# Causal masks of two heads in one operation, with a new written order, in a decay attention with a gated MLP

## The chip, the cores and the metric

The kernel runs on one core of one Trainium2 chip. The metric is device time in microseconds (us) of one launch, median of repeated runs.

## What is computed

Attention with a decay over 8 batches of 8 heads (sequence S = 576, head size D = 64), then an MLP on the heads put side by side (512 columns) that is gated by a causal convolution of 5 taps:

```python
log_f = np.log(np.clip(f, 0.0001, 1.0))
cum = np.cumsum(log_f, axis=-1)
decay = cum[:, :, :, None] - cum[:, :, None, :]
scores = np.where(causal, -1000000000.0, scale * q @ k.T + decay)
attn = np.exp(scores - max); attn = attn / (sum + 1e-09)
x = (attn @ v) of all heads, as (batch, 576, 512)
...
gate_pre[s] = sum over k of conv_w[k] * x[s - 4 + k]
out = (sigmoid(gate_pre) * (x @ w_val)) @ w_out
```

(The listing is shortened: q, k, v, x and f are inputs, `max` and `sum` run over a row of scores, `causal` is the part above the diagonal.)

## The kernel before

**Work.** Two heads make a pair; there are 32 pairs (i = 0 to 31), four to a batch. The 576 rows of scores of a head are cut into four blocks of 128 (j = 0 to 3; block j has 128(j+1) columns because of the causal mask) and a tail of 64 rows, which the two heads of a pair share as one block of 128 rows ("l"). For each pair the steps are:

- Scores on PE (helper `mm`, line 246), in three groups: blocks 3 and 2 of both heads, blocks 1 and 0, the tail. From pair 4 on q and k are split in a rounded high part Xh (line 261) and a rest Xl (line 375), and three products are added.
- The decay of a head, one row of 512 numbers, is read from a small table in DRAM and broadcast to 128 partitions, into one of four tiles dm (two pairs' worth); the tail has its own tile dl. The mask is put into the same tile: of the last 128 columns of block j (128j to 128j+127) those above the diagonal get a large negative number. Lines 468 (POOL, affine_select) and 470 (DVE, an addition of the constant tile tri4, in the rows tri) are this step, one operation for each head and block. The step of block j overwrites columns that block j+1 reads unmasked. So it comes after the reduction of block j+1 of that head.
- Line 459, DVE: a custom reduction adds dm to the scores in PSUM and finds the row's extreme, negm. Line 463, ACT: the exponential, with its row sums zs. Lines 477 and 478, DVE: 1/z for the pair.
- Line 503, PE: transposes of the probabilities in three groups (block 3; blocks 2 and 0; block 1); line 527: those of the tail, with 1/z in the same operation. Copies to SBUF by ACT or DVE (helper, line 261).
- 1/z goes out to DRAM (rzd, issued by SP on line 272) and comes back, broadcast to 64 partitions for each head, into one of three tiles x32.
- Products with V on PE, in two halves; line 577, DVE: each half times 1/z in x32, in place. That is x of the MLP.
- x is split in xh (line 261, ACT or DVE) and xl (line 584, POOL or DVE). The convolution is a first product (line 266, 267 or 268, on ACT, POOL or DVE) and four taps (line 619, DVE); for the first four pairs a tap may be on POOL instead, as a product (line 268) and an addition (line 617). Then a tanh for the gate on ACT.
- Per batch: products with w_val (PE), line 651 the gate times the product into h (DVE), its split hh and hl (lines 261 and 665), products with w_out (PE), line 692 (ACT) or 694 (DVE) to an output tile ot (two of them), and the store.

The start loads and cleans up the weights (a decode in integers on DVE and ACT) while the first pairs run.

**Order.** Nothing runs in the order of this code. Each step is put as a node into `Plan` with the engines that may run it and a cost for each; `Plan.order` then goes through a long string, TABLE (lines 46 to 106), that holds for every node in turn its number, its engine and its PSUM banks (eight of 512 columns). The order of each engine's queue, the engine of each step with a choice, and each bank are thus written out in TABLE; the costs in the code take no part when the kernel is built. The waits between engines follow from the tiles.

The node of the mask, in `plan_s`:

```python
any_("sel", {"POOL": 0.26, "DVE": 0.3}, pp - (0.3 if j == 3 else 0.0), sel, [*dkey, ("tri4",)], dkey)
```

Of the kernel before, what the change touches and what calls it, by code (L numbers as in the profile page):

```python
# [7 lines left out]
F32 = mybir.dt.float32  # L8
# [3 lines left out]
ALU = mybir.AluOpType  # L12
# [4 lines left out]
P = 128  # L17
# [5 lines left out]
L0 = NB * P  # L23
# [8 lines left out]
BIG = 8.0e9  # L32
# [5 lines left out]
NDM = 4  # L38
# [8 lines left out]
0430520q000930240010b30n010l000m010d30a30630e20f10740z40K40g10h20r30i20p000C228001232a02900V40B10D20E22j0450F10G20H20t32R40I20J20c32h22i12d22b22s062m2  # L47
2k20M12f22e10j40N22t02c10o002n12q22644642l12g12o22u22r12D0210x32p12F22x0054042v12A0434245f42E20w30P22B10Q12z12w20O22C12V012672X00R22G030S22W03222y1302
340050U32-22Y23924442H13522Q10X13-42T43315h42K45d40T12Z12_10s33110y33d030Y20-23e00_12I42M42O43724a33b20u33k020Z23f21021125q33c13613g13813i063a13A0055b
44c23l23x0233C13j23h23D045943B13u0063y24843z13m15l33v11333o33E13p23q23r23w14f31211444b023174d23N14o0064i34g21610v34B041f43F44e13Q024l34j24p34m21724s34  # L50
h14k14n14q23H44v34r14t24C24u14y33L43J43O014D17844z27e44L0734A14w24F0454x14M13R24H13P23s24N14E24O063n31821925n37c43S14G13U34P17n13T37l35m050123V23W25o2
4I0435r24S47g44Y15t34K15z0677t35w34J15u21a15x24Q47a45A35s15y15M034W44Z005B25N24U45p18n45D35C15v15O15E24_051b25J25K25G35L15F13X25Q0125H21c25025W0735I17
m34-21d21i25S15P25Y15Z023Y28A18p47o31e31h11k27q35335437p006545j47k36715-18B27r21j25X15T0237w35R17u25_48C37z31l16145525V17x26547A26341m28v47C0715627s15
U11q45113t17v16a037y168027D37B13Z17T0607U15727P048r41n27V16b26928F37E25236e17Q26c16f26g26h27i48D31p37R17J28t47K29C48I37F17G38E063206d36n046k057H21s11o
# [12 lines left out]
hd2h93gp4cF04h41cG0hl05cC1ha2jY4e82hi3hb1iP4fm2iR4cH2hm2cD4g-1j22hj2gw02he1hk1hf3hg2hn1hh1fk2cI4k24gx2gu04e53gv2hp013hv056hs002cK04cL0hr1hu2e92ho2ea2h
y02hq1ht1iZ3fn2hw1i-05017hz2hI2cM1i_3k04hA4j32cN4kb3j02j52j82hx1j62iV2jc2gy1j11gA1hC4jb023hE4kc3k93kh3gB2j92jf3jd2hG4cP06eb1j41ji3cQ0jo04j71jp2cU00jg2
ja1jq1je1cR2fo2jj2jl3hJ07hL06jm2gC2jn1jk1gz3js024hK2jh1jy037jv051gD2jw1hM2jA2ju1jr2jt1ka2lb4j-4hP1jz1jx2hN1fp2k44iT4hV06ke3hO3cV0lq3jB01jC2kd03457hQ2k
f2ki2gE2jL1cW1kn3kq012hY00hZ0kj1lj4ko2kk3lf4hW0lo1lw3ku3i104kg1mq4kl2kr2ks2jD4hR2km1jF4kp1h-2i20kv2hX2jJ4i405kx2gF1ky2h_1fq1i50k83hS2ms4jH4kD06jM00hT2  # L70
kE2i02lp3k64kz1kw1i32i62lr3jO03ld4mD3kt1kF1lh4kA2kB2kH046kC1kN057kJ1mF1i901jP2i72ia0kI1jN2lt3cX4ln2i82kK006kO1kL1ib2kG2mu4ls05423kP2kQ00ic07cS4lx2kR1l
u2kU4lC3jQ2id0k-1ly1lv1lS00lz3ie2lF075lA2if1lD2l104lG3lJ2lB1mE2lK2lT2hU1lP2my4kM1mG2lQ2lU1ig2kS4kW4k_06lH2mI2jS3ih02lR1lM3ii0lE1jR3oy4lN2ij2lI1lL1kY4i
k03il0lW025m0001lO1l02lZ067im2lX1jT2oC4in1ip02ll4jU2l22lV2l-1oN3m11m303m22lY1io3m41mL2mH05106oG4md1mw4oO2mM2m74mU034oL1mN1oT3mJ2mR2mC2iq0l_2mS2mK1l51o
A4mO3mY3mP2iu01mT1l62mZ2n22mQ1mV3jV2ir1mW2iz07pN4l72n505m54is4m_3mX1q02m94oE4iv0iw2m-1n62n32mb4me02n41mg01n71n02jW2n9040nf056oM3nb1oQ3mf2mh2na2iA0n11n
h1q13nc063mk1oP04012l82l32ng1iB2mA4n82p-3oK3nd1ml2ni05oR2ne1ns1p0037nj2oW2l43oU2oX2oS1pT4pd05oZ2ix4o-2p13p43mi1pP4nk4iE04oY1p52pe2o_1oV1nm4pa3pR4pf1iF
0p22pb2mj3p31p73q63nq4mm2p61no4p82nt00r84nu2pc1p91nv05ph030iG2pg2nw2pn047r64pV4nx2pq05mn2ny2pk021po2p_3mo2jX1q33pj1pp1pA1nF07pr1nG0pm1q201456nH2qf070l
92q42q72pl1pi1nI03q92nz1q81qa2qc2q51qd2nJ0nA2qb1qg3nN02nK2iC4qh2la1qi1nL1qj3nO0oI4qs04r24r04nQ03mp1qk2sf4qp2pZ2nB2qe1r44nM2rf3nP2nR0ps4qm3pu4pw4pB01qq
2qr1ss2rg3ql1qn2py4rl3qt2pC2pD02pE2qC006qo1qu1ra4qw017qz045qv2nS2qD2qA2sh4pX4qF02rd3re3qy1nV07pH3qB1iH4rc3qx1st3qG2nT1nU3rh01450qP2ri3su2ru023nC2nW0rm
# [12 lines left out]
A-1CP3CQ2AX1BQ053CD4AW1B14BI2BF2DQ4BN2BO2BU3zh07BK3zp04zq0zi0wL1BL2BG1z81BP1BR3BV2ug4BS2B-3B34B_2BM1zj2BX3xX2BW1zm02zk2C100xY2BJ1By3CW3zn0BY2B74C01C22
# [76 lines left out]
def tile_decay_attention_gated_mlp(  # L168
# [27 lines left out]
    def tiles(n, shape, dt, name):  # L196
        return [const.tile(shape, dt, name=f"{name}{j}") for j in range(n)]
# [626 lines left out]
```

## Time and profile before

| | us |
|---|---|
| median of 3 runs | 571.55 (569.11 to 572.59) |
| profiled execution, its own time | 567.13 |
| its span | 565.4 |
| busy: PE, DVE, ACT, POOL | 501.1, 479.9, 342.9, 241.8 |
| mean granted clock, share of full speed | 0.954 |

All durations come from the one profiled execution. The rows are in a section below; a row gives a line of the kernel before, the engine, the operation, the tiles by name (written <- read), and its times. A wait of an engine is idle time just before an instruction, with what released it. Two engines are busy for more than four fifths of the span, so the shares do not name one bound, and the stretches and waits are to be read.

### The profile page before, as it was taken

The numbers are of one execution on the slowest core, as the hardware profiler recorded it, in microseconds if no ns is written. First come the engines' busy times: TensorE is split into PE (matmuls) and PEld (weight loads), VectorE is DVE, ScalarE is ACT, GpSimd is POOL, SyncE is SP. The second block draws the span as 40 slices with busy tenths as digits, with TensorE's granted clock in tenths as the row PEclk, the third lists the DMA queues.
The fourth block names the chain that finished last, engine by engine and source line by source line (L and its number), as shares of the span: only waits on it lengthen the run. The fifth ranks groups of instructions, "written<-read, shape, count | busy, mean of one in ns | idle before, by whom it ended". The sixth has DMA issues, their size and how long they took to land. (4 is left out here: it accounts for less than half of the span.)

```text
span 565.4 us, 14142 instructions
## 1 busy us (share of the span) xinstructions
PE 501.1 (89%) x5136; PEld 429.3 (76%) x5136; DVE 479.9 (85%) x1204; ACT 342.9 (61%) x933; POOL 241.8 (43%) x352
## 2 busy tenths in 40 slices
PE   7877897897889998999988989989899778999997
PEld 6655786776888878878877778977798666988795
DVE  5879979989689998889888799898979868987871
ACT  5877756766657666766746556655655545677321
POOL 3337854637272716245463334252434345442000
PEclk9988769999799999999989989989989989999999
DMA  6763634545353653544642754446444345522112
GB/s 236 195 231 122 179 132 128 155 139 200 94 158 117 172 168 118 173 132 137 200 137 83 186 141 139 140 118 194 131 132 122 90 149 152 182 88 69 60 39 93
DMA packets 35014, 79.58 MB, mean 141 GB/s; under 512 B 5056, under 2 KB 5312, under 8 KB 34944
## 3 DMA queue, kind: packets, MB, share of 16 engines
q1 hardware_dynamic: 34864, 78.54, 45.4%
q8 instruction: 40, 0.66, 0.5%
q14 instruction: 30, 0.25, 0.1%
q10 hardware_dynamic: 80, 0.15, 0.1%
HBM read 68.93 MB, written 9.73 MB: 139 GB/s over the span
## 5 line engine op out<-in xcount | busy, mean ns | idle before, releaser
L463 ACT ACTIVATE P<-banks,negm 128x384 f32<-128x384 f32 (+3 forms) x256 | 133.4, 529 | 97.6 <-DVE negm L459 94.7
L468 POOL TENSOR_SCALAR_AFFINE_SELECT dm<-dm 128x128 f32<-128x128 f32 x169 | 60.6, 367 | 189.9 <-DVE negm L459 153.1
L459 DVE CUSTOM_DVE_ANT_0 banks<-banks,dm 128x512 f32<-128x512 f32 (+2 forms) x240 | 115.2, 508 | 16.6 <-POOL dm L468 7.1
L619 DVE SCALAR_TENSOR_TENSOR gate<-x,cw,gate 128x576 f32<-128x576 f32 x126 | 123.5, 985 | 0.6
L246 PE MATMUL banks<-xh,wall 128*128 128x288 f32 x512 | 116.3, 309 | 6.0 <-DVE h L651 1.9
L246 PE MATMUL banks<-pt,vt 128*64 128x128 f32 (+1 forms) x1280 | 100.5, 311 | 16.6 <-ACT ot L692 7.1
L261 ACT COPY pt<-banks 128x512 f32<-128x512 f32 (+1 forms) x173 | 85.8, 540 | 42.9 <-PE banks L503 27.3
L246 PEld LDWEIGHTS banks<-pt,vt 128*64 128x64 f32 x1280 | 80.9, 145 | 29.8 <-ACT P L463 8.1
L246 PEld LDWEIGHTS banks<-xh,wall 128*128 128x128 f32 x512 | 87.4, 194 | 11.2 <-DVE h L651 2.4
L246 PE MATMUL banks<-wall,hh 128*128 128x512 f32 x288 | 92.8, 403 | 2.6 <-ACT ot L692 1.4
L246 PE MATMUL banks<-xl,wall 128*128 128x288 f32 x256 | 77.2, 301 | 0.0
L503 PE MATMUL banks<-ident,P 64*128 64x64 f32 x1280 | 56.3, 235 | 17.5 <-ACT P L463 9.9
L375 POOL TENSOR_TENSOR Xl<-Xr,Xh 128x640 fp32r<-128x640 f32 (+1 forms) x43 | 68.7, 1604 | 2.8 <-DVE Xh L261 2.6
L503 PEld LDWEIGHTS banks<-ident,P 64*128 64x128 f32 x1280 | 48.5, 146 | 27.5 <-ACT P L463 15.4
L246 PEld LDWEIGHTS banks<-wall,hh 128*128 128x128 f32 x288 | 51.0, 188 | 14.9 <-ACT ot L692 1.5
L246 PE MATMUL banks<-Xh 64*128 64x512 f32 (+3 forms) x224 | 54.3, 381 | 5.5 <-DVE x L577 2.4
L246 PE MATMUL banks<-wall,hl 128*128 128x512 f32 x144 | 56.6, 393 | 0.0
L463 ACT ACTIVATION_READ_ACCUMULATOR P<-banks,negm 128x1 f32 x256 | 51.9, 203 | 0.0
L246 PEld LDWEIGHTS banks<-xl,wall 128*128 128x128 f32 x256 | 49.8, 195 | 0.1
L246 PE MATMUL banks<-Xl,Xh 64*128 64x512 f32 (+3 forms) x224 | 49.7, 346 | 0.0
L246 PE MATMUL banks<-Xh,Xl 64*128 64x512 f32 (+3 forms) x224 | 49.6, 345 | 0.0
L577 DVE TENSOR_TENSOR x<-banks,x 128x192 f32<-128x192 f32 (+1 forms) x64 | 27.7, 449 | 17.6 <-DMA x<-rzd 13.4
(102 smaller groups left out, 794.0 us busy)
## 6 DMA issues: line engine op xcount, KB each, us to landing
Xr<-in_x_dram SPq DMA_DIRECT2D x32, 608.0 KB
dm<-decd SPq DMA_DIRECT2D x60, 256.0 KB
vt<-in_v_dram SPq DMA_DIRECT2D x32, 320.0 KB
x<-rzd SPq DMA_DIRECT2D x64, 144.0 KB
out_dram<-ot SPq DMA_DIRECT2D x36, 256.0 KB
dl<-decd SPq DMA_DIRECT2D x60, 144.0 KB
ot<-in_w_val_dram SPq DMA_DIRECT2D x2, 512.0 KB
wu<-in_w_val_dram SPq DMA_DIRECT2D x2, 512.0 KB
```

Of the source, the lines that this page charges most:

```text
L246: nc.tensor.matmul(out, lhsT=lhsT, rhs=rhs, start=start, stop=stop)
L261: (eng.copy if eng is nc.scalar else eng.tensor_copy)(out=out, in_=in_)
L375: eng.tensor_tensor(out=Xl[r][:, a:e], in0=Xr[r][:, a:e], in1=Xh[r][:, a:e].bitcast(F32), op=ALU.subtract)
L459: nc.vector.tensor_tensor_reduce(out=sl, in0=sl, in1=add, op0=ALU.add, op1=ALU.min, scale=-0.125, scalar=3.0e38, accum_out=negm[r][:, col])
L463: nc.scalar.activation(out=dst[:, o:o + ext], in_=bank(key)[:, c0:c0 + ext], func=AF.Exp, bias=negm[r][:, col], scale=-1.0, accum_out=zs[r ...
L468: eng.affine_select(out=t, in_=t, pattern=[[-1, P]], base=0, channel_multiplier=1, compare_op=ALU.is_ge, fill=-BIG)
L503: nc.tensor.transpose(out=bank(key[a])[:, c:c + D], in_=Pt[ms[h]][sl, BOFF[b] + P * j:BOFF[b] + P * j + P], identity=ident[sl, sl])
L577: nc.vector.tensor_tensor(out=o, in0=bank(key)[:, 0:qb - qa], in1=o, op=ALU.mult)
L619: eng.scalar_tensor_tensor(out=gt, in0=src, scalar=wt_, in1=gt, op0=ALU.mult, op1=ALU.add)
```

## The change

1. The four decay tiles of 512 columns become two tiles of two heads each. One operation puts the mask of block j into both heads: 128 partitions by 2x128 columns. It waits until the reductions of block j+1 of both heads have been made.
2. Two costs that the planner knows are changed (the mask, the transposes). They take no part when the kernel is built.
3. The whole of TABLE is another: order, engines and banks.

```diff
-    dm = tiles(NDM, [P, L0], F32, "dm")
+    dm2 = tiles(NDM // 2, [P, 2, L0], F32, "dm")
+    dm = [dm2[m // 2][:, m % 2] for m in range(NDM)]
...
-                if u < 2 and not deep:
-                    def sel(eng, t=dm[md][:, ext - P:ext]):
+                if u < 2 and not deep and h == 0:
+                    def sel(eng, t=dm2[i % (NDM // 2)][:, :, ext - P:ext]):
                         if eng is nc.gpsimd:
-                            eng.affine_select(out=t, in_=t, pattern=[[-1, P]], base=0, channel_multiplier=1, compare_op=ALU.is_ge, fill=-BIG)
+                            eng.affine_select(out=t, in_=t, pattern=[[0, 2], [-1, P]], base=0, channel_multiplier=1, compare_op=ALU.is_ge, fill=-BIG)
                         else:
-                            eng.tensor_tensor(out=t, in0=t, in1=tri4, op=ALU.add)
-                    any_("sel", {"POOL": 0.26, "DVE": 0.3}, pp - (0.3 if j == 3 else 0.0), sel, [*dkey, ("tri4",)], dkey)
+                            eng.tensor_tensor(out=t, in0=t, in1=tri4[:, None, :].to_broadcast([P, 2, P]), op=ALU.add)
+                    dk2 = [("dm", (2 * i + q) % NDM) for q in range(2)]
+                    any_("sel", {"POOL": 0.36, "DVE": 0.34}, pp - (0.3 if j == 3 else 0.0), sel, [*dk2, ("tri4",)], dk2)
...
-            pe("PT", 0.058 * 2 * nt + 0.02, p, go, [("ident",), *(("P", m, b) for m in ms for b in blocks)], key, cols=256 * nt, mode=1)
+            pe("PT", 0.0622 * 2 * nt, p, go, [("ident",), *(("P", m, b) for m in ms for b in blocks)], key, cols=256 * nt, mode=1)
```

Of TABLE, the first line:

```diff
-0430520q000930240010b30n010l000m010d30a30630e20f10740z40K40g10h20r30i20p000C228001232a02900V40B10D20E22j0450F10G20H20t32R40I20J20c32h22i12d22b22s062m2
+0b30z40010240630B10430E20o000930F10r30740e20C20K40520m010q000n010D20f10h20G20l000H20I20i20d30j40p010a32R428010232j0452a00V40c32904044640t30J20M10g10N2
```

In numbers of instructions: masks on DVE 71 of one head, after it 62 of two; on POOL 169 and 58. First products on DVE 2 and 13, taps on DVE 126 and 121, products and additions of taps on POOL 2 and 7 of each. Output tiles on DVE 13 and 7. Casts of h to hh on DVE 15 and 31 (of these 5 and 11 have 64 columns); of the other copies, casts and subtractions on DVE that have changed engine, 24 fewer. PE has 4318 matmuls and transposes in both, SP 361 issues in both.

In the middle of the program, before, PE runs the last rows of a value product, then the V product of pair 21 (tiles pt, pl, vt), then the transposes of pair 22 (P to banks):

```order
L246 MATMUL banks<-xh_101,wall 128x288
L246 MATMUL banks<-xl_107,wall 128x288
L246 MATMUL banks<-xh_101,wall 128x288
L246 MATMUL banks<-pt_87,vt_91 64x128 x12
L246 MATMUL banks<-pt_87,vt_91 64x192 x8
L246 MATMUL banks<-pl_89,vt_91 64x64 x2
L503 MATMUL banks<-ident,P_83 128x64 x8
L503 MATMUL banks<-ident,P_81 128x64 x8
L503 MATMUL banks<-ident,P_83 128x64 x4
L503 MATMUL banks<-ident,P_81 128x64 x4
L503 MATMUL banks<-ident,P_83 128x64 x8
L503 MATMUL banks<-ident,P_81 128x64 x8
```

The tail scores of pair 22 stand just ahead of these rows. After the change, at the like place, on PE:

```order
L503 MATMUL banks<-ident,P_80 128x64 x8
L503 MATMUL banks<-ident,P_81 128x64 x8
L245 MATMUL banks<-Xh_75 128x512 x2
L245 MATMUL banks<-Xh_75,Xl_77 128x512 x2
L245 MATMUL banks<-Xl_77,Xh_75 128x512 x2
L245 MATMUL banks<-Xh_75 128x384 x2
L245 MATMUL banks<-Xh_75,Xl_77 128x384 x2
L245 MATMUL banks<-Xl_77,Xh_75 128x384 x2
L503 MATMUL banks<-ident,P_80 128x64 x4
L503 MATMUL banks<-ident,P_81 128x64 x4
L245 MATMUL banks<-pt_84,vt_88 64x192 x8
L245 MATMUL banks<-pl_86,vt_88 64x64 x2
```

These are transposes of pair 23, the first score group of pair 24 (Xh, Xl), the transposes of block 1 of pair 23, and then the V product of pair 22. The V product has moved behind work of the next two pairs.

On DVE, before, the chain of reductions (ISA rows with two tiles; the row with 128x1 reads its result out) and masks (L470); dm_69 and dm_70 are the two heads of a pair:

```order
L459 ISA banks,negm_92<-banks,dm_69 128x512
L459 ISA negm_92 128x1
L261 COPY pl_89<-banks 73x128
L470 TENSOR_TENSOR dm_69<-dm_69,tri_66 128x128
L459 ISA banks,negm_92<-banks,dm_70 128x512
L459 ISA negm_92 128x1
L459 ISA banks,negm_92<-banks,dm_69 128x384
L459 ISA negm_92 128x1
L470 TENSOR_TENSOR dm_70<-dm_70,tri_66 128x128
L459 ISA banks,negm_92<-banks,dm_70 128x384
L459 ISA negm_92 128x1
```

After the change, where dm_70 is the tile of both heads:

```order
L458 ISA banks,negm_91<-banks,dm_70 128x512
L458 ISA negm_91 128x1
L458 ISA banks,negm_91<-banks,dm_70 128x512
L458 ISA negm_91 128x1
L469 TENSOR_TENSOR dm_70<-dm_70,tri_66 128x2x128
L477 TENSOR_SCALAR Pl_82<-zs_92 128x9
L478 RECIPROCAL Pl_82<-Pl_82 128x9
L458 ISA banks,negm_91<-banks,dm_70 128x384
L458 ISA negm_91 128x1
```

The mask stands once, behind both heads' reductions of block 3 (512 columns), and ahead of both reductions of block 2; the reciprocal has moved in between.

On POOL, in the start of the program, before: a low part of the weights (wall), the first product of the convolution of pair 0, and masks of pair 2:

```order
L745 TENSOR_TENSOR wall<-gate_113,wu 128x512
L268 TENSOR_SCALAR gate_112<-x_96,cw 128x576
L468 AFFINE_SELECT dm_70<-dm_70 128x128
L468 AFFINE_SELECT dm_69<-dm_69 128x128
L361 MEMSET x_97 128x4
L468 AFFINE_SELECT dm_70<-dm_70 128x128
L468 AFFINE_SELECT dm_69<-dm_69 128x128
L468 AFFINE_SELECT dm_70<-dm_70 128x128
L468 AFFINE_SELECT dm_69<-dm_69 128x128
L468 AFFINE_SELECT dm_70<-dm_70 128x128
```

After the change POOL takes all four taps of pair 0 itself, each as a product (h_112) and an addition:

```order
L267 TENSOR_SCALAR gate_110<-x_94,cw 128x576
L360 MEMSET x_96 128x4
L267 TENSOR_SCALAR h_112<-x_94,cw 128x576
L617 TENSOR_TENSOR gate_110<-gate_110,h_112 128x576
L267 TENSOR_SCALAR h_112<-x_94,cw 128x576
L617 TENSOR_TENSOR gate_110<-gate_110,h_112 128x576
L267 TENSOR_SCALAR h_112<-x_94,cw 128x576
L617 TENSOR_TENSOR gate_110<-gate_110,h_112 128x576
L267 TENSOR_SCALAR h_112<-x_94,cw 128x576
L617 TENSOR_TENSOR gate_110<-gate_110,h_112 128x576
L745 TENSOR_TENSOR wall<-gate_111,wu 128x512
L584 TENSOR_TENSOR xl_104<-x_94,xh_98 128x576
```

The masks that stood there are fewer and further behind.

## Rows read from the trace of the kernel before

**Rows 1.** Page: span; busy us, share of the span and instructions of each engine

```profile
span 565.4 us, 14142 instructions
...
PE 501.1 (89%) x5136; PEld 429.3 (76%) x5136; DVE 479.9 (85%) x1204; ACT 342.9 (61%) x933; POOL 241.8 (43%) x352
```

**Rows 2.** Stretches: stretch, length, busy PE, PEld, DVE, ACT, POOL; PEclk, DMA share, GB/s

```profile
30.00:100.00 70.00, 55.53 (x544) 46.78 (x540) 62.88 (x141) 48.70 (x130) 42.71 (x55) 0.83 0.49 156
100.00:500.00 400.00, 359.72 (x3826) 310.36 (x3826) 351.64 (x894) 243.64 (x676) 178.16 (x247) 0.97 0.48 143
500.00:540.00 40.00, 38.39 (x400) 33.64 (x399) 31.29 (x76) 23.28 (x62) 10.49 (x16) 1.00 0.23 74
```

**Rows 3.** Waits of DVE: engine, tile, line <- releaser: us in total, times, longest us

```profile
DVE x L577 <- DMA x<-rzd: 13.4, 9, 2.5
DVE h L651 <- PE banks L246: 7.8, 5, 3.5
DVE banks L459 <- POOL dm L468: 7.1, 15, 0.8
```

**Rows 4.** Timeline of DVE at the last pair's reciprocal and product: start us, us, operation

```profile
523.36 0.22 DVE L478 RECIPROCAL Pl<-Pl 128x9 f32<-128x9 f32 x1
...
533.88 0.82 DVE L577 TENSOR_TENSOR x<-banks,x 128x192 f32<-128x192 f32 x2 [2.50 <-DMA x<-rzd]
```

**Rows 5.** Chain that ended last, 520 to 536 us: start us, us, piece

```profile
526.86 1.71 DMA rzd<-pl
...
529.97 3.79 DMA x<-rzd
```

**Rows 6.** Waits of PE, same columns as rows 3

```profile
PE banks L503 <- ACT P L463: 9.9, 10, 3.1
PE banks L246 <- ACT ot L692: 8.6, 4, 4.1
...
PE banks L527 <- DVE Pl L478: 5.2, 6, 2.1
```

**Rows 7.** Groups by shape, costliest first: operation and count | busy us, mean ns | idle before

```profile
L619 DVE SCALAR_TENSOR_TENSOR gate<-x,cw,gate 128x576 f32<-128x576 f32 x126 | 123.5, 985 | 0.6
...
L468 POOL TENSOR_SCALAR_AFFINE_SELECT dm<-dm 128x128 f32<-128x128 f32 x169 | 60.6, 367 | 189.9 <-DVE negm L459 153.1 <-DMA dm<-decd 30.5 <-DVE dm L470 3.0
...
L375 POOL TENSOR_TENSOR Xl<-Xr,Xh 128x576 fp32r<-128x576 f32 x21 | 33.1, 1577 | 0.1
...
L470 DVE TENSOR_TENSOR dm<-dm,tri 128x128 f32<-128x128 f32 x71 | 32.8, 465 | 0.6
...
L694 DVE TENSOR_SCALAR ot<-banks 128x512 f32<-128x512 f32 x13 | 8.8, 684 | 7.2 <-DMA out_dram<-ot 6.6 <-PE banks L246 0.6
...
L261 DVE CAST xh<-x 128x576 fp32r<-128x576 f32 x14 | 8.8, 625 | 0.1
...
L617 POOL TENSOR_TENSOR gate<-gate,h 128x576 f32<-128x576 f32 x2 | 3.3, 1646 | 0.8 <-DVE gate L619 0.8
...
L268 POOL TENSOR_SCALAR h<-x,cw 128x576 f32<-128x576 f32 x2 | 2.7, 1371 | 0.0
...
L268 DVE TENSOR_SCALAR gate<-x,cw 128x576 f32<-128x576 f32 x2 | 2.2, 1112 | 0.0
...
L261 DVE CAST hh<-h 128x512 fp32r<-128x512 f32 x5 | 2.1, 422 | 0.0
...
L322 POOL TENSOR_SCALAR_AFFINE_SELECT gate<-gate 128x192 f32<-128x192 f32 x2 | 0.7, 348 | 0.1
```

**Rows 8.** Line 470 in the whole trace: duration ns min/median/max, first and last start

```profile
L470 DVE TENSOR_TENSOR dm<-dm,tri x71: 231/291/1532, 25.5 to 514.9; 128x128 f32<-128x128 f32 x71
```

**Rows 9.** Timeline of POOL and DVE around 205 us

```profile
204.32 1.42 POOL L584 TENSOR_TENSOR xl<-x,xh 128x576 fp32r<-128x576 f32 x1
...
204.45 1.90 DVE L619 SCALAR_TENSOR_TENSOR gate<-x,cw,gate 128x576 f32<-128x576 f32 x1
...
206.73 0.81 DVE L619 SCALAR_TENSOR_TENSOR gate<-x,cw,gate 128x576 f32<-128x576 f32 x1
```

More of the change, by code (lines that the diff above doesn't have):

```diff
@@ L51 @@
[L51 to L54, printed above, removed]
@@ L103 @@
[L103 to L104 removed]
+0b30z40010240630B10430E20o000930F10r30740e20C20K40520m010q000n010D20f10h20G20l000H20I20i20d30j40p010a32R428010232j0452a00V40c32904044640t30J20M10g10N2
+0O20P20Q12k22l12m22f22o22g12h22q22p12i12b20R20s30S22d22s062t02n12u22r12D0342c10x32E1340522F12A0430T22e13923a12x0013522B22z22C14243615b42645d44442v12V0
@@ new lines @@
+34510U30X10Y23722w23b20-22G064a31442H12y10Z22W02X02I40y30_12Q22K43-43c12-21022_13d062Y22O43e02Z13811211123u0343023w11333221613k023112M41f43i043f21724c
+31921a13313A0503v11821b20u32T43x0133l23j20v33C13B13g11c23z13y11e21h14b040251d25943h21i24f23D064d24h23E15744m0134k24i25544n23N14q24o23H44s24x064g13F44e
+17044v24t24l14B0403O054j13o34r14y24p11k24w14D15h24u14z10w33p33L43J44H0231l15j24I24E0104G13Q063q31j24F17243m17645i010271m24A23r34841n21o17d24J11q47f14C
+13R23P23s31p34K055m27443S15E034U15k25o24L15r25l15p25F27e25n13n33U35u35q17845t0565I0015G15x25K14M45v25z25C27g35J15s14O45w15D11s18b47h034215A23V27i37j27
@@ new lines @@
+l25y14S44V074Q47n25B17q27o21t24X003T37k17m13W37p15O0358o37t38p35H23X28j44Y27s0467u25P15Q15R024W25S17w25L0505_17D025M17r17x11u27c27y37E25N17H0573Y27v11
+v24_38h45f48f47z28d45V45T47B29m45X45025127F18q37J14Z17A17C17G260007I18r38s072318t37N0643t18w28x162058u25Z48y29q47O11B48z28B26c026128v17Q067P18n39s4632
+7K0408A16427-18E26527a49o48D0538H27R14-38O068F28P28C17M19B18S0018J28I18T19z38K29A36d05237L28M26638Q15328G19C38N16729E39D006748L18U18V0539H21w18W19F29J
+29K27_019u47U49M27S41x2ax4aB47Y48R28X1az481039G16f006839y26923Z19L17W46g09I11z11y29P3aK38_058029N19O0479918229016a28l4a1031a216h26e28Y0561E29S29Q29U2c
@@ new lines @@
+B4aM19146n008Z29X29348-19Z026k066i26l01A31D19V29-2aF4aP3cF49R16j26s056o09T16m29Y18531G21F29w4541aD4aL3aN39W1a31cJ4954a40616p29749_1a02862cQ3aO02347aS2
+aQ2aU2872aV2a51a7060cH46t01M4cD46q1a81aR19a06a61aX26r31H16u29c02a91aT18311I2aW19d29b2cR3aa00aZ0536v02a-3b12a_2ak16w0aY1882b336x2ab16y26b18921J2b8009g3
+b426D026A076E0cO1aJ39e1b01b62b92b51cN26B06z2dM4aH46C2b216F2cP39h2b71bf0351L36G2cT3ae4ac4ba1bc001cS02746bh1dS4dU4ai4ag4bb2be1bg1cU2bi015cW28a11X4cY2bj1
+bd1bk1d_3cZ2c_2an03d22cV1d1050d52bl01cX1e03al07bm2dQ4d32bv19i2d72dZ3dc01dO4d01da2843bn46H3ao2c-1d411O1dg046dd2am2bw03d82d611R2bp4eX4br49j2dh1bt4cL4de1
@@ new lines @@
+d919k2db1di1d-3e101274dj060df2e23e32e52by05ap1e41dl1dk1dp00e72ea29f3e82dq2bx2dY3eb1e61bz2e91bA2aq31K2bI06en03eZ4f34eo2dz1er072fa3et1f83ec001ed3bB2ee2e
+_4dt4dr4dx4ep1es1dm052do2eg2ei2bJ0fb3ef1ej2f93fc07234eh1dn1dv4ek1bK21P2el21Q2em1fd3fe2eq2fg2ex0561S1dC009l1fi2fj2dA01ez1fh16X02dW41T2dB2ey2dD2eA051U2f
+f1fl2fk1g64eK1fn003gc4fo2eu017g84eB2fr2ga41V1ge41W26N05fp2bL06dG2bM0ev1fs1f146I011Z1fm11-2202gj3ft3fq1fu2f736S041_2211222ew2bQ07dH2241232252dI26O0bN2f
+w2bC16P16J0ar2fx16K1fy05i74as2fv1bD26Y0at2fz2bO2bT00f54gl3bU0i54eE4fA1bR06L4eC46T0fC056au2fD1av2gi3gm3bP2fF013gk3bV2ii3bS2bE2ib4go3b_07bY05aw1c00fE2ik
@@ L105 @@
+IO2IP1DZ1Fp1IX05IQ3J603Je04HK2IR3Jm01IY0I_0E500IZ2Gz2J02Ea02J70IS2E34HL1IT2J11GA1IU2Eb0J40J22J52Jc0J82Jf0E60IV2J92Ja2Jn0Jj03Jk0Jg2IW1Jd2Jh2Ec2Ji2Jw02J
+r06Jo2Jl2Jp2Jq2D-4Js0JB03Jx0JC0JL01E71E84Ed4Jt1JG06Jy2Ju4JH0Jz4JD1JI1JE4JJ4JM0JN1JO4
 """
```

89 lines of the change are left out of this document (36 added, 53 removed).

## The prediction, made before the changed kernel ran

> **What bounds the kernel now.** I read the page first, then the busy time by stretches, then what each engine waited for, then the chain of waits at the end, then single operations by shape. The page gives a span of 565.4 us; TensorE (PE) is busy for 501.1 us of it and VectorE (DVE) for 479.9 us [rows 1]. Two engines are nearly full, so the stretches decide. From 30 to 100 us DVE is busy 62.88 of 70 us and PE 55.53; from 100 to 500 us PE has 359.72 of 400 and DVE 351.64; from 500 to 540 us PE has 38.39 of 40 [rows 2]. PE stands still for 14.5 + 40.3 + 1.6 = 56.4 us between 30 and 540 us, and DVE for 64. No engine alone sets the time. Each chain of a pair of heads passes scores on PE, the row minimum on DVE, the exponential on ScalarE (ACT), transposes on PE, copies, products with V on PE. The time beyond PE's work is what these engines wait for one another, so a new order can win up to the waits it removes, and lose as much by new ones.
>
> The longest wait of DVE is for a transfer: nine times, 13.4 us in all, line 577 (the product of the attention output with 1/z) stood until 1/z had come back from DRAM. Next are the value product, 7.8 us, and the masks made by GpSimd (POOL), 7.1 us in 15 times [rows 3]. The tail shows the first: the reciprocal of the last pair begins at 523.36 us, line 577 begins at 533.88 after 2.50 us of idle time [rows 4]. So the round trip needs about 10.5 us; of it the write took 1.71 us and the read with broadcast 3.79 [rows 5]. PE's own long waits are for exponentials before transposes (9.9 us), for an output tile (8.6 us) and for the reciprocal before the last transposes of a pair (5.2 us) [rows 6].
>
> **The change, part by part.** *Work.* Of the 240 masks of one head, 71 ran on DVE and 169 on POOL; now 62 of two heads run on DVE and 58 on POOL. Before, DVE paid 71 x 0.465 = 33.0 us and POOL 60.6 [rows 7]. No operation of 2x128 columns is in this trace. On DVE it lies between 0.465 (start-up dominates, columns are free) and 0.93 (two old ones); I take 0.60, nearer to the single one, since the single one is 0.291 in the median against a mean drawn up by a few of up to 1.532 [rows 8]: 62 x 0.60 = 37.2, so +4 us, with ends at -4 and +25. On POOL the select of 192 columns took 0.348 and two old masks take 0.734; I take 0.45: 26.1 us, so -34.5 (ends -40 and -18).
>
> Other engines are given other work, counted row by row in the new order. DVE gets 11 more first products of the convolution (2 to 13): at the 0.625 of a cast of that size +6.9 us, at the 1.112 of its own two old rows +12.2. It loses 5 taps, 5 x 0.985 = -4.9. It gains ten big casts of the gated product at 0.422, +4.2 (six of 64 columns are left out), and loses 24 other copies, casts and subtractions, priced between the 0.625 of a cast and the 0.684 of an output evacuation: -15 [rows 7]. Together DVE comes out at +4.2 + 6.9 - 4.9 + 4.2 - 15 = about -5 us, with the unknown ends between -13 and +21. POOL loses 34.5 us of masks and gets five more multiply-and-add pairs, 5 x (1.371 + 1.646) = +15.1, and some seven more long subtractions at 1.58, +11 [rows 7]: -8. PE does the same 4318 matmuls and transposes, and the 361 DMA issues of SP (SyncE) are the same in number: nothing there.
>
> *Order of the chain.* Before, PE does the V product of pair i ahead of pair i+1's transposes. After, it does most of pair i+1's transposes and the first scores of pair i+2 ahead of it. So between the reciprocal of a pair and its line 577 more DVE work stands. Summed with mean durations of the rows, the DVE work in that gap is 11.8 us in the mean of the 32 pairs before, under the round trip of 10.5 in ten; the trace has nine waits, which agrees [rows 3]. After, the mean is 17.3 us and one pair is under 10.5. That takes away some 11.5 of the 13.4 us; 2 are left for the first pair and for late writes. PE's wait for the reciprocal shrinks too, since the transposes of the last block come later behind the second score block (median 8.1 us of PE work against 6.2): half of 5.2, about -2.5.
>
> *Mask chain.* A mask of a block may only go in when the rows of the block above it have been reduced, for both heads now. Before, 124 times a POOL mask stood between two DVE reductions of its own pair, 28 of them with under 0.7 us of DVE work as cover; after, 38 times, 11 with little cover. POOL's mask waits of 7.1 us [rows 3] fall by the same share: -4. The new wait, for the second head, is hidden where the other head's reduction runs anyway; behind a waiting mask POOL's queue holds long subtractions, for which the split of the pair after next waits, and behind a mask on DVE nothing waits, because the reductions ahead of it are on DVE itself.
>
> *What is lost.* Between the first score block of a pair and its transposes there were under 5.5 us of PE work in four pairs; now in twelve. PE will wait there for exponentials; the wait of this kind is 9.9 us in ten times [rows 6], so eight more at half of 1 us: +4. The start decodes a weight tile ahead of the first reductions: +1. The last stretch keeps its length: PE has 243 matmul instructions behind the last transposes, 219 before, and from 534.30 us on PE runs without a break in the profile.
>
> *Sum.* -11.5 - 2.5 - 4 - 5 + 4 + 1 = -18 us of waits and work, on DVE and PE both. PE was idle for 56 us against DVE's 64, so not every wait of one engine was the end's: I count half, -9 us. The profiled execution takes 567.13 us against a span of 565.4; 567.1 - 9 = 558. The median of the three runs shown is 571.55, 4.4 us above the profiled one. I put the forecast to the median: 571.55 - 9 = 562.
>
> **A rule against this change.** DVE's tap at 204.45 us took 1.90 us while POOL subtracted from 204.32 to 205.74; the next tap, alone, took 0.81 [rows 9]. So a POOL operation costs a two-input DVE operation up to 1.1 us. The Trainium skill, page "SBUF — State Buffer", section "Who interferes with whom", says why: an instruction of DVE with two SBUF inputs shares a read port with a POOL instruction that reads SBUF, and whoever comes first keeps the other out for its whole length. By that rule the tap should have waited for POOL's end at 205.74 and ended at 206.55; it ended at 206.35, so the trace agrees nearly. The rule would make DVE's masks, which have two inputs, and the new POOL pairs dearer; what it gives is the third rival.
>
> **Rivals.**
> 1. *The deeper order pays in full.* PE's 56 us of idle time [rows 2] fall by half, because the V product no longer holds the transposes of the next pair up. For it: DVE's longest wait goes away as a kind. Against: DVE is itself at 88% from 100 to 500 us. Time: 571.6 - 28 = about 544.
> 2. *Waits move and do not shrink.* The lines for an output tile (8.6) and for exponentials (9.9) [rows 6] are not touched by the change and take what line 577 gives back; the masks are hidden anyway. For it: two engines at 88 to 90% of a stretch leave little room. Time: 571, give or take 4.
> 3. *The start slows.* Between 30 and 100 us DVE is busy 62.88 of 70 us and the granted clock is 0.83 [rows 2]. The new order puts four multiply-and-add pairs of POOL in a row there, 3.0 us each [rows 7], and a fifth behind; these are 15 us in which DVE's two-input operations can be held, at 0.75 to 1.1 us each meeting [rows 9]. Ten to fifteen meetings give +8 to +15 us, less the 4 us of taps saved; where DVE is full that goes to the end one to one. With a both-head mask at 0.93 (+20 on DVE) it is slower in the rest as well. It decides if the gain in waits is under 10 us. Time: 571.6 + 8 = about 580.
> That the masks do not become fewer cannot be: the counts are in the program.
>
> **How the numbers follow.** Forecast (552 to 568, most likely 562): 0.40. Rival 1: 0.12. Rival 2: 0.25. Rival 3: 0.23, because I can count the meetings only roughly. A measurement of this kernel tells about 1% from no change, 5.7 us: faster is below 565.8, slower above 577.3. Faster: 0.38 of the forecast's and all of rival 1, 0.50. Same: rival 2 and the forecast's upper edge, 0.27. Slower: 0.23. The range for 8 in 10 is 545 to 578: it takes in the forecast and rival 2 whole, the lower half of rival 3's spread and the edge of rival 1, and the ends of the mask's price (DVE -4 to +25 us, half of it felt).
>
> **What would show it.** In the profile of the changed kernel DVE's wait of line 577 for the read of 1/z should be at 2 to 4 us in place of 13.4; DVE's wait for POOL's masks at 3 in place of 7.1; the two-head mask at about 0.60 us on DVE and 0.45 on POOL; DVE's busy time within 10 us of 479.9. PE's wait of line 503 for exponentials should rise from 9.9 to about 14. The tap's mean at or under 0.985 speaks against rival 3, over 1.1 for it. The forecast is wrong if line 577 still waits over 8 us, if PE's idle time between 30 and 540 us does not fall from 56 us to about 47, or if the stretch from 30 to 100 us ends later by more than 5 us.

## The result, and the profile after

The changed kernel takes 540.91 us (540.05 to 542.29, four runs) against 571.97 for the kernel before: ratio 0.947, 95% interval 0.943 to 0.951. Measured twice more, on two chips, it took 541.21 and 542.45 us, with ratios of 0.956 (0.950 to 0.963) and 0.958 (0.954 to 0.963): the kernel before was faster there (567.60 and 565.75 us), since it varies more between chips and runs than this one. I had forecast 562, with a range of 545 to 578. The sign was right; the gain, 31 us, is more than three times the 9 us forecast, and the time lies below the range.

The page's head:

```profile
span 538.2 us, 13925 instructions
...
PE 488.6 (91%) x5136; PEld 421.8 (78%) x5136; DVE 479.0 (89%) x1193; ACT 338.3 (63%) x924; POOL 241.1 (45%) x257
```

Beside [rows 1]: the span is 27.2 us shorter and DVE's busy time is the same (479.9, now 479.0). Told from DVE, nearly all of the gain is idle time, 85.5 us before and 59.2 now. Told from PE, it is 14.7 us of idle time (64.3, now 49.6) and 12.5 us of busy time, with the same 5136 records; what PE's clock has to do with that is asked below. The stretches, with the columns of [rows 2]:

```profile
30.00:100.00 70.00, 55.31 (x598) 44.57 (x596) 65.13 (x163) 49.86 (x143) 47.65 (x44) 0.88 0.63 171
100.00:500.00 400.00, 372.23 (x4111) 326.48 (x4108) 373.49 (x927) 258.31 (x712) 179.66 (x177) 1.00 0.48 146
```

DVE stood still for 48.4 us between 100 and 500 us; now for 26.5. From 30 to 100 us it is 7.1 and 4.9 us. Between 30 and 500 us it does 24 us more work than before. PE's granted clock is at its full level nearly all of the time from 100 us on, where it had been 0.97 in the mean. The waits of DVE:

```profile
DVE h L651 <- PE banks L245: 9.4, 7, 5.8
DVE ot L694 <- PE banks L245: 5.0, 2, 4.3
...
DVE banks L458 <- POOL dm L467: 2.7, 7, 0.5
DVE x L577 <- PE banks L245: 2.2, 4, 0.8
...
DVE Pl L477 <- ACT P L462: 1.2, 1, 1.2
```

The wait of line 577 for 1/z, 13.4 us in [rows 3], stands nowhere in the list any more; the one for POOL's masks fell from 7.1 to 2.7. Two waits that the rows ahead of the prediction do not show have also shrunk. Before, they were:

```profile
DVE ot L694 <- DMA out_dram<-ot: 6.6, 2, 4.4
DVE Pl L477 <- ACT P L463: 4.4, 4, 2.3
```

Of PE's waits in [rows 6], the one for exponentials ahead of transposes, which I had let grow from 9.9 us to 14, is 9.0; the one for the reciprocal fell from 5.2 to 0.5; the one for an output tile, 8.6, is gone from the list:

```profile
PE banks L503 <- ACT P L462: 9.0, 11, 1.9
...
PE banks L527 <- DVE Pl L478: 0.5, 1, 0.5
```

The operations, by shape, and the mask of two heads by its spread (columns as in [rows 7] and [rows 8]):

```profile
L619 DVE SCALAR_TENSOR_TENSOR gate<-x,cw,gate 128x576 f32<-128x576 f32 x121 | 118.8, 992 | 0.5
...
L469 DVE TENSOR_TENSOR dm<-dm,tri 128x256 f32<-128x256 f32 x62 | 38.7, 626 | 1.1
...
L267 DVE TENSOR_SCALAR gate<-x,cw 128x576 f32<-128x576 f32 x13 | 8.2, 628 | 0.0
```

```profile
L467 POOL TENSOR_SCALAR_AFFINE_SELECT dm<-dm 128x256 f32<-128x256 f32 x58 | 34.3, 592 | 132.0 <-DVE negm L458 103.1 <-DMA dm<-decd 17.1 <-DVE Pl L477 7.5
```

```profile
L469 DVE TENSOR_TENSOR dm<-dm,tri x62: 408/426/1641, 34.3 to 485.6; 128x256 f32<-128x256 f32 x62
```

The end of the chain (start, us, piece), first before, then after:

```profile
524.91 0.55 PE banks L503 x13
...
534.30 27.60 PE banks L246 x150
```

```profile
491.14 1.42 PE banks L503 x40
492.56 0.31 PE banks L527 x10
492.87 41.83 PE banks L245 x286
```

The last pair's transposes end 32.6 us earlier (525.5, 492.9); behind them the time to the end is 39.9 us before and 45.3 now, where the chain is PE's products without a break until 534.70. So 32.6 us were won up to there and 5.4 given back at the end.

### The profile page after: what moved, and what is told of

It reads as the page before. It is cut to its first block, busy times and chain, and to the rows that moved or that the text cites. A ratio compares the mean times of both kernels' runs of the same rounds, so it can differ in the third digit from the quotient of the medians.

```text
span 538.2 us, 13925 instructions
## 1 busy us (share of the span) xinstructions
PE 488.6 (91%) x5136; PEld 421.8 (78%) x5136; DVE 479.0 (89%) x1193; ACT 338.3 (63%) x924; POOL 241.1 (45%) x257
## 5 line engine op out<-in xcount | busy, mean ns | idle before, releaser
L462 ACT ACTIVATE P<-banks,negm 128x256 f32<-128x256 f32 (+3 forms) x256 | 134.3, 530 | 70.7 <-DVE negm L458 69.3
L458 DVE CUSTOM_DVE_ANT_0 banks<-banks,dm 128x512 f32<-128x512 f32 (+1 forms) x240 | 114.7, 506 | 10.4 <-POOL dm L467 2.7
L619 DVE SCALAR_TENSOR_TENSOR gate<-x,cw,gate 128x576 f32<-128x576 f32 x121 | 118.8, 992 | 0.5
L245 PE MATMUL banks<-pt,vt 128*64 128x128 f32 (+1 forms) x1280 | 96.5, 304 | 1.4 <-ACT P L462 1.2
L467 POOL TENSOR_SCALAR_AFFINE_SELECT dm<-dm 128x256 f32<-128x256 f32 x58 | 34.3, 592 | 132.0 <-DVE negm L458 103.1
L245 PEld LDWEIGHTS banks<-xh,wall 128*128 128x128 f32 x512 | 85.5, 189 | 8.3 <-ACT P L462 2.8
L374 POOL TENSOR_TENSOR Xl<-Xr,Xh 128x576 fp32r<-128x576 f32 (+1 forms) x47 | 75.3, 1607 | 11.3 <-ACT Xh L260 8.5
L245 PE MATMUL banks<-Xh 64*128 64x512 f32 (+2 forms) x224 | 54.1, 383 | 10.4 <-ACT pt L260 2.8
L245 PEld LDWEIGHTS banks<-xl,wall 128*128 128x128 f32 x256 | 48.4, 189 | 1.9 <-DVE xl L584 1.3
L584 POOL TENSOR_TENSOR xl<-x,xh 128x576 fp32r<-128x576 f32 x24 | 37.6, 1568 | 26.0 <-ACT xh L260 16.6
L245 PE MATMUL banks<-Xh,Xl 64*128 64x512 f32 (+2 forms) x224 | 47.9, 336 | 0.4 <-DVE Xl L374 0.4
L245 PE MATMUL banks<-Xl,Xh 64*128 64x512 f32 (+2 forms) x224 | 47.3, 332 | 0.0
```

Source lines behind the costliest of these rows:

```text
L245: nc.tensor.matmul(out, lhsT=lhsT, rhs=rhs, start=start, stop=stop)
L374: eng.tensor_tensor(out=Xl[r][:, a:e], in0=Xr[r][:, a:e], in1=Xh[r][:, a:e].bitcast(F32), op=ALU.subtract)
L458: nc.vector.tensor_tensor_reduce(out=sl, in0=sl, in1=add, op0=ALU.add, op1=ALU.min, scale=-0.125, scalar=3.0e38, accum_out=negm[r][:, col])
L462: nc.scalar.activation(out=dst[:, o:o + ext], in_=bank(key)[:, c0:c0 + ext], func=AF.Exp, bias=negm[r][:, col], scale=-1.0, accum_out=zs[r ...
L467: eng.affine_select(out=t, in_=t, pattern=[[0, 2], [-1, P]], base=0, channel_multiplier=1, compare_op=ALU.is_ge, fill=-BIG)
L584: any_("xl", {"POOL": 1.4, "DVE": 0.67}, p, lambda eng: eng.tensor_tensor(out=xl[s], in0=xv, in1=xh[s][:, :].bitcast(F32), op=ALU.subtract ...
```

## The experiments

The table puts the profiled executions side by side. DVE idle is span less busy. The clock is the mean share of full speed that was granted. Each ratio is to the kernel before on the same chip. The spans are of single executions on several chips (the other executions of the kernel before were granted 0.955 to 0.982, so its profile is one of low clock): where span and ratio differ, the ratio is the better measure.

| kernel | span | PE busy | DVE busy | DVE idle | clock | median us | ratio (interval) |
|---|---|---|---|---|---|---|---|
| before | 565.4 | 501.1 | 479.9 | 85.5 | 0.954 | 571.97 | 1 |
| after | 538.2 | 488.6 | 479.0 | 59.2 | 0.981 | 540.91 | 0.947 (0.943 to 0.951) |
| after_unfused | 548.2 | 493.0 | 491.0 | 57.2 | 0.974 | 546.42 | 0.967 (0.960 to 0.975) |
| before_fused | 560.9 | 491.5 | 467.8 | 93.1 | 0.982 | 562.95 | 0.995 (0.991 to 1.000) |
| after_engB | 582.5 | 505.0 | 476.3 | 106.2 | 0.953 | 584.97 | 1.033 (1.025 to 1.041) |
| before_engA | 581.6 | 503.4 | 469.9 | 111.7 | 0.962 | 583.61 | 1.032 (1.025 to 1.039) |
| before_rz | 554.6 | 496.0 | 481.3 | 73.3 | 0.969 | 558.50 | 0.988 (0.982 to 0.994) |
| before_ot4 | 564.4 | 497.9 | 482.7 | 81.7 | 0.973 | 564.84 | 0.995 (0.992 to 0.999) |
| before_all3 | 557.0 | 493.4 | 468.4 | 88.6 | 0.975 | 559.19 | 0.986 (0.980 to 0.993) |
| before_fill | 561.2 | 500.6 | 480.8 | 80.4 | 0.982 | 568.08 | 1.001 (0.997 to 1.006) |
| after_fill | 542.1 | 492.9 | 479.0 | 63.1 | 0.980 | 544.58 | 0.962 (0.957 to 0.967) |
| after_again | 538.2 | 486.1 | 477.5 | 60.7 | 0.987 | 541.21 | 0.956 (0.950 to 0.963) |
| before_dve | 581.4 | 502.9 | 513.6 | 67.8 | 0.964 | 588.21 | 1.039 (1.031 to 1.047) |
| after_dve | 570.2 | 501.5 | 512.8 | 57.4 | 0.964 | 573.24 | 1.013 (1.005 to 1.020) |
| after_maskP | 540.7 | 490.4 | 463.4 | 77.3 | 0.977 | 540.39 | 0.955 (0.948 to 0.963) |
| after_mask3 | 541.3 | 486.7 | 477.6 | 63.7 | 0.984 | 542.92 | 0.960 (0.956 to 0.964) |
| after_mask30 | 544.3 | 490.2 | 466.4 | 77.9 | 0.975 | 544.29 | 0.963 (0.959 to 0.966) |
| after_third | 541.6 | 489.7 | 478.2 | 63.4 | 0.977 | 542.45 | 0.958 (0.954 to 0.963) |

**The joint mask by itself.** The changed kernel with two operations in the place of one:

```diff
-                            eng.affine_select(out=t, in_=t, pattern=[[0, 2], [-1, P]], ...)
+                            for q in range(2): eng.affine_select(out=t[:, q], in_=t[:, q], pattern=[[-1, P]], ...)
-                            eng.tensor_tensor(out=t, in0=t, in1=tri4[:, None, :].to_broadcast([P, 2, P]), op=ALU.add)
+                            for q in range(2): eng.tensor_tensor(out=t[:, q], in0=t[:, q], in1=tri4, op=ALU.add)
```

> The changed kernel with its own order, engines and banks; only the mask of both heads is two operations of 128 columns again, in the same place and on the same engine. Theory A (the order made the gain, the joint mask is a small part): 62 times on DVE two of about 0.3 to 0.465 us in place of one of 0.626, so -2 to +19 us on DVE; time 543 to 553 us. Theory B (the joint mask made the gain): 558 us or more, most of the 31 us given back.

546.42 us, as theory A expects: 4 to 5.5 us of the gain are given back by the medians, 10.0 by the profiled spans (this profile is of the slowest of its four executions, 549.9 us). DVE's work rose by 12.0 us (479.0 to 491.0):

```profile
L470 DVE TENSOR_TENSOR dm<-dm,tri 128x128 f32<-128x128 f32 x124 | 56.0, 492 | 0.6
```

Its idle time hardly changed (57.2). So order, engines and banks without the joint mask give 0.967, the joint mask the rest, one to two per cent.

The reverse, the joint mask in the order of before:

```diff
 # table of before: of the two mask steps of a block the second is kept, as one operation on both heads;
 # the 42 reductions, 13 exponentials and 2 loads that stood between are put behind it
```

> The kernel before, its order, engines and banks, with the joint mask of 2x128 columns put where the second head's mask stood (a few reductions and exponentials move behind it): 120 masks in place of 240, 32 on DVE and 88 on POOL. Theory A: 566 to 575 us, since DVE saves about 71 x 0.465 - 32 x 0.626 = 13 us of work but waits longer for POOL's masks. Theory B: 545 to 560 us.

562.95 us lies between the two theories' times, but these were put for a kernel before of 571.6 us, and it took 566.78 on this chip. As ratios, A expects 0.990 to 1.006 and B 0.953 to 0.980; measured was 0.995, in A's range. DVE's work fell by 12.1 us and its idle time rose by 7.6: in this order more than half of the work saved turned into waiting, since the reductions now wait 21.7 us for POOL's masks in place of 7.1 [rows 3]:

```profile
DVE banks L458 <- POOL dm L467: 21.7, 40, 2.0
```

**Order or engines.** Each swap changes the engine of 263 steps (mostly copies, casts, subtractions, first products, output tiles) and leaves the order and the banks:

```diff
 # in TABLE, for each step that is no mask: its engine digit
-engine of the changed kernel
+engine of the kernel before          (after_engB; before_engA the other way round)
```

> The changed kernel with its order and banks, but each of the 263 steps that changed engine is back on its engine of before (the masks keep theirs). Theory A: the order carries the gain alone, 541 to 552 us. Theory C (the division of work among the engines made the gain): 556 us or more.

> The kernel before, its order and banks and its masks of one head, with each of the 263 steps on the engine that the changed kernel gives it. Theory A: no gain without the order, 566 to 580 us. Theory C: 556 us or less.

Both became 3% slower than the kernel before. For after_engB that is what theory C said, for before_engA it is above both theories' numbers, so neither theory is right for the two: the order without its engines loses, the engines without their order lose. In before_engA the reductions on DVE wait longer for POOL's masks (7.1 us before) and for PE's scores (3.0 before):

```profile
DVE banks L459 <- POOL dm L468: 13.2, 15, 5.1
DVE banks L459 <- PE banks L246: 12.2, 15, 1.8
DVE x L577 <- DMA x<-rzd: 10.3, 10, 2.8
```

Line 577 still waits 10.3 us for 1/z there, and in after_engB this wait is not in the list: the new order, with its banks, took it away, the new engines did not. The banks went with the order in every run, and what they give alone was not tried.

**The named waits in the order of before.**

```diff
-            load("rzr", 0.65, p + 0.04, x32[...][...], rzd[i, h:h + 1].to_broadcast([D, S]),
+            load("rzr", 0.65, p + 0.04, x32[...][...], decd[2 * i + h:2 * i + h + 1].to_broadcast([D, S]),
```

> The kernel before; the factor that line 577 multiplies with is read from the decay table in DRAM, written once at the start, in place of the pair's own 1/z, so the read need not wait for the write (1/z is still computed and written; the product is with other numbers). DVE's wait of 13.4 us in line 577 should be near 0. Theory A1 (a wait of DVE counts in full, and PE's clock rises with it): 571.6 - 11 to - 16, 556 to 561 us. The step of the prediction (half of it counts): 563 to 567 us. Theory A2 (other waits take its place): 569 us or more.

The wait did not go to zero:

```profile
DVE x L577 <- DMA x<-decd: 6.2, 7, 1.8
```

The read is still issued behind the write in SP's queue, and only 7.2 of 13.4 us went. The ratio 0.988 is 7.0 us at 568, with an interval of 3.7 to 10.3: about the whole of 7.2 us. Half of it, 3.6 us, lies just outside the interval, so my price of one half is not borne out for this wait, though not by much.

```diff
-    ot = [otw[:, n] for n in range(2)]
+    ot = [otw[:, n] for n in range(2)]; ot += [wu[1].bitcast(F32)[:, DM * n:DM * n + DM] for n in range(2)]
-        ot[n % 2], key ("ot", n % 2)
+        ot[n % 4], key ("ot", n % 4)
```

> The kernel before with four output tiles in place of two (two more in a weight buffer that is idle by then). The waits for the store (DVE 6.6 us, ACT 2.6, PE 8.6 behind ACT's evacuation) should go. Theory A1 (full price): 561 to 566 us. If they only move: 569 us or more.

DVE's wait for the store is gone, and 0.5% with it (0.1 to 0.8). DVE's idle time fell by 3.8 us out of 6.6 (85.5, 81.7): before the same operations DVE now waits 6.2 us for PE's results, 0.6 before, and PE's wait for an output tile fell from 8.6 to 5.7.

All three edits at once:

> The kernel before, its order and engines, with three edits at once: joint mask, line 577's factor read from other data (not from the pair's own 1/z), four output tiles. Alone they gave ratios of 0.995, 0.988 and 0.995 to before. If the waits are independent: product 0.978, about 559 us for 571.6. If the changed kernel's gain is these waits and no more: 0.947. If they replace one another: 0.985 or more.

0.986, interval 0.980 to 0.993, the same as the factor of line 577 alone. That speaks for edits that replace one another in the old order, but does not show it: the product 0.978 has an interval of its own (an estimate from the three: 0.970 to 0.986), and the two overlap. DVE does 11.5 us less work than before and stands idle 3.1 us more, with 22.1 us of waits for POOL's masks as in before_fused. What is shown is that these three edits are not what made the changed kernel: 1.4 of its 4.2 to 5.3%.

**Is PE's clock a cause?** In the profile of before, PE's clock was granted at its lower level (1.2 of 2.4 GHz) for 0.046 x 2 x 565 = 52 us; now for 0.019 x 2 x 538 = 20. It fell after a long pause of PE: from 138.7 to 142.76 us PE waited for an output tile to be emptied, and the stretch from 140 us has a mean of 0.66:

```profile
142.76 0.70 PE L246 MATMUL banks<-pt,vt 128*64 128x128 f32 x4 [4.09 <-ACT ot L692]
```

```profile
140.00:150.00 10.00, 7.24 (x88) 6.66 (x88) 6.80 (x17) 5.93 (x17) 3.28 (x4) 0.66 0.30 77
```

I filled such pauses with transposes of the identity (73 of them in before_fill and 41 in after_fill; the expectations say 77 and 40):

```diff
+FILL = {244: (8, 384), 317: (6, 384), ...}     # step: transposes, first column in its bank
+            if n in FILL:
+                yield partial(self.fill, nd["take"][0], *FILL[n]), e
             yield nd["fn"], e
```

> The kernel before, with 77 transposes of the identity added to PE at 13 places, right ahead of a step for which PE stood still by 1.2 to 3.1 us in the trace, into columns of that step's own bank that it does not use or overwrites. Theory K (the pauses of PE cost twice, since the granted clock falls to half after them, and this clock is a cause of the time): time at the low clock falls from 52 us to under 30, and the kernel is 5 to 12 us faster than before although PE has more to do. Theory A (the other engines' waits set the time, PE's clock only follows): the clock may rise, the time stays within 3 us or is longer.

> The changed kernel with 40 such transposes at 8 places (pauses of 1.1 to 2.5 us, 44 to 135 us). Theory K: time at the low clock from 20 us to under 10, 2 to 5 us faster than the changed kernel. Theory A: same within 2 us.

The mean clock over all runs rose from 0.965 to 0.976, the time did not change: 1.001 (0.997 to 1.006). In the changed kernel the same filling cost 3.4 us and did not raise the clock (0.980 in the mean, 0.982 without). Raised for itself, with the work that this takes (12.2 us of PE in before_fill), the clock gave nothing back here. A fill that costs nothing was not tried: in before_fill the added transposes themselves waited 8.0 us at four places for their bank.

```profile
PE banks L775 <- ACT P L467: 8.0, 4, 3.1
```

But the clock can be held equal without a fill. Executions of the kernel before that were granted 0.976 to 0.982 took 560.2 to 566.9 us; executions of the changed kernel that were granted 0.971 to 0.975 took 541.0 to 542.4. And before_fused, granted 0.982 in its profile with PE busy for 491.5 us, close to the changed kernel's 488.6, has a span of 560.9. So the higher clock, and PE's shorter busy time with it, can be worth a part of the gain, but 18 us or more of it are there at the same clock.

**The price of DVE's work.** One more addition of 128x320 behind each product of line 577:

```diff
                 nc.vector.tensor_tensor(out=o, in0=bank(key)[:, 0:qb - qa], in1=o, op=ALU.mult)
+                nc.vector.tensor_tensor(out=scr, in0=scr, in1=scr, op=ALU.add)
```

> The changed kernel with one more operation of DVE behind each of the 64 products of line 577: an addition of 128x320 columns in a scratch tile that nothing reads (some 0.45 us by the rows of 128x384 and 128x192, 29 us in all). Theory D (in the new order DVE has little idle time left and each us of its work costs nearly one; in the old order other waits take half of it up): +20 to +29 us here, 561 to 570 us. If DVE has slack: under +12.

> The kernel before with the same 64 additions. Theory D: the price of DVE work is about half, as the joint mask showed in this order (12 us less work, 4.5 us less span in the profiles): +10 to +18 us, 580 to 588 us. If the price is the same in both orders: +20 to +29 us.

DVE's busy time rose by 33.8 us in the one and 33.7 in the other. The changed kernel became 32.0 us longer by the spans, 31 to 32 by the medians and some 33 by the ratios (1.013 less 0.954, the mean of its three): each us of added work cost 0.9 to 1 us. The kernel before became 21.9 us longer by the ratio (interval 17 to 26): a price of 0.5 to 0.8. The spans give it 16.0, but its profile is of the fastest of its four executions. Its idle time took up the rest, 85.5 us before and 67.8 with the additions. Both numbers are above theory D's ranges, and the second lies where the rival put it; what is left of theory D is that the same work costs some 10 us more in the new order, with intervals that about meet (the first ratio's own spread, 1.005 to 1.020, is 9 us wide). The first row is after_dve's page, the second before_dve's:

```profile
PE 501.5 (88%) x5136; PEld 428.9 (75%) x5136; DVE 512.8 (90%) x1258; ACT 339.2 (59%) x924; POOL 244.4 (43%) x257
```

```profile
PE 502.9 (86%) x5136; PEld 426.1 (73%) x5136; DVE 513.6 (88%) x1269; ACT 342.4 (59%) x933; POOL 245.2 (42%) x352
```

**Less work for DVE.** In TABLE, DVE's masks are given to POOL: every second one, those of block 3, those of blocks 3 and 0.

```diff
-    if e == "DVE" (62 masks)
+    e = "POOL"   # after_maskP: every second; after_mask3: block 3 (10); after_mask30: blocks 3 and 0 (25)
```

> The changed kernel with every second of DVE's 62 joint masks on POOL, at the same place of the order. DVE loses 31 x 0.626 = 19 us of work, POOL gains 31 x 0.592 = 18 us and has room (45% busy). If POOL's masks are hidden there: 525 to 532 us, better than both kernels. If the reductions behind each moved mask now wait for it (0.6 us and a hand-over each way): 540 to 555 us.

> The changed kernel with DVE's ten joint masks of block 3 on POOL, same place in the order. A mask of block 3 waits for no reduction, only for the decay's load. DVE loses 10 x 0.626 = 6.3 us. Theory D with hidden masks: 6 us less, 535 us (ratio to the changed kernel 0.989). If POOL's long subtractions ahead of them make the first reduction wait: 541 us or more.

> The same with the 15 DVE masks of block 0 on POOL as well: DVE loses 25 x 0.626 = 15.7 us. Theory D with masks hidden: 526 to 530 us. If the hand-over to POOL and back costs what DVE gives up, as in the kernel with every second mask moved: 540 us.

None is better than the changed kernel (0.955, 0.960 and 0.963 against its 0.947 to 0.958). With every second mask moved DVE had 15.6 us less work and 18.1 more idle time; the reductions now waited for POOL:

```profile
DVE banks L458 <- POOL dm L467: 13.9, 25, 1.7
```

The masks of block 3, which wait for no reduction, brought nothing either (542.92 against 542.45 on the same chip): the ten masks left DVE, but its work fell by only 0.6 us against after_third, since other operations became longer (the taps by 2.2 us in all, line 477 by 1.5), and its reductions of fresh scores waited 5.8 us for PE in place of 4.9. The two comparison runs took 541.21 and 542.45 us:

> The changed kernel once more, on the same chip as the three others, for comparison: ratio 0.947 to before by its first measurement.

> The changed kernel on the same chip, for comparison: 540 to 542 us.

## Why the prediction was wrong

- *The step that failed* is the last of the sum: "PE was idle for 56 us against DVE's 64, so not every wait of one engine was the end's: I count half, -9 us." With the sizes that its terms turned out to have (13.4, 4.7, 4.4, 0.9 and 0.9 us, as the next points say) the sum is -24; half of that is -12, and the gain was 31 us by the medians and 27.2 by the spans. Half is near the price that before_dve measured for DVE's time in the old order (0.5 to 0.8); in the new order after_dve measured 0.9 to 1. As these two runs put it, the price changed with the order, and I carried one price over. At full price the sum as worked out, -18, would have given 554; what is missing from there to 541 are the terms below that were too small or left out.
- *Line 577*: right. I took away 11.5 of 13.4 us; all 13.4 went, by the order with its banks, as before_engA and after_engB show.
- *The reciprocal ahead of the last transposes*: right in kind, too small. I took off half of 5.2 us; 4.7 went.
- *Masks made by POOL*: -4 forecast, 7.1 to 2.7 measured. Right.
- *DVE's work*: -5 forecast, -0.9 measured. The joint mask took 0.626 us against 0.60 taken; on POOL 0.592 against 0.45, outside neither bound. The first product was 0.628, at the lower of my two values. Taps rose from 0.985 to 0.992. The casts of the gated product added 7.4 us, not 4.2.
- *PE's work* was put at nothing, since its instructions are the same in number. Its busy time fell by 12.5 us, with 32 us less at the low clock: the counts hold, the durations do not.
- *Exponentials*, +4: wrong in sign; 9.9 became 9.0 [rows 6]. I counted PE's work between the first scores and their transposes only. DVE now reduces with fewer waits and may release the exponentials earlier; no run shows that this is the reason.
- *Left out*: PE's wait for an output tile (8.6 us, gone), DVE's for the store of one (6.6 us, in part replaced by 5.0 for PE's results), line 477's for exponentials (4.4 to 1.2). Rival 2 said in so many words that the change would not touch the first.
- *The last stretch keeps its length*: it grew by 5.4 us. That the new order has 24 more matmul instructions there was counted, and given no price.
- *Rival 1* came near the time (544) by luck: PE's idle time from 30 us to the end of the steady part fell from 56 to 42.5 us, by a quarter and not by half. The rest of PE's share is busy time, and DVE's idle time fell by about twice as much (26.3 us). Its reason against, DVE at 88% from 100 to 500 us, was no bound: DVE went to 93%.
- *Rival 3*: the start did not slow; DVE was busy for 65.13 of 70 us in it (62.88 before), and the taps all but kept their mean.
- *DVE's masks beside POOL*: the joint mask's median is 0.426 us, its mean 0.626. One took 1.44 us while POOL, which had begun first, subtracted from 480.28 to 481.70:

```profile
480.28 1.42 POOL L584 TENSOR_TENSOR xl<-x,xh 128x576 fp32r<-128x576 f32 x1 [1.45 <-ACT xh L260]
480.55 1.44 DVE L469 TENSOR_TENSOR dm<-dm,tri 128x256 f32<-128x256 f32 x1
```

By the rule of the Trainium skill, page "SBUF — State Buffer", section "Who interferes with whom", that a DVE instruction with two SBUF inputs is kept out for the whole of a POOL instruction that reads SBUF and came first, the mask would begin at 481.70 and, with its median, end at 482.13 (an estimate). It ended at 481.99, so the trace agrees nearly. This did not decide the time. If all of the difference between mean and median is put down to POOL, it is 62 x (0.626 - 0.426) = 12 us for the joint masks, and the old ones paid as much, 71 x (0.465 - 0.291) = 12 us.

What stays open: order, engines and banks give 3.3% without the joint mask, while two named waits and the joint mask, taken care of in the old order, give 1.4% together. Where the rest of the 3.3% comes from, many small waits or PE's clock in part, no run here separates.

## What to carry to other kernels

Where two engines are near full, compare each one's busy time with the span before and after: here DVE's busy time did not move, so the gain had to be in its waits. What DVE's time is worth can differ between orders: the same added work cost 0.5 to 0.8 of itself in the old one and 0.9 to 1 in the new one, so a price read from the old order need not hold for the new. In an order written out by hand, engine and place of a step are one choice; changing 263 engines alone cost 3% in the old order and 8% in the new one. Work taken off the fullest engine counts only if its hand-over costs less than the work.

## What the runs showed of the hardware

- One operation of 2x128 columns is cheaper than two of 128: on DVE 0.426 us in the median against 2 x 0.291 (means 0.626 and 2 x 0.465); on POOL 0.412 in the median against 2 x 0.295 (means 0.592 and 2 x 0.367).
- After a pause of PE of 4.09 us the granted clock had a mean of 0.66 over the next stretch of 10 us. More work of PE in such pauses raised the clock of the kernel before (0.965 to 0.976 in the mean of the runs) and won no time; in the changed kernel it did not raise it.
- A DVE addition of 2x128 columns took 1.44 us beside a POOL subtraction that had begun first, against 0.426 in the median.
- The time of the kernel before spread over 560 to 573 us on the chips used, that of the changed one over 539.8 to 543.9.
